# Opening loads: the first gate weights on ScalarE's DMA queue behind a memset, both first x tiles on SyncE's

## The chip, the cores and the metric

One core of a Trainium2 chip; the three sets of experiments ran on three different chips, each set with the kernel before beside it. The metric is the device time of one execution in microseconds (us). The span in a profile, first to last instruction, is about 1.8 us shorter than the time of the same execution. Medians and numbers of runs are given; where a ratio is given, it is the mean time of one kernel's fast runs over that of the other's of the same rounds, so not quite the ratio of the medians. A tile is 128 rows of x. A transfer is issued when the engine named starts it on its queue, and has landed at the last of its completion events in the trace.

## The reference

```python
xn = layernorm(x)                                  # x: 2048 x 640
g  = silu((sigmoid(xn @ w_gate) * (xn @ w_up)) @ w_down)   # F = 1536
s  = attention(xn @ wq, last 512 of k_cache, v_cache) @ wo # 32 heads of 192
return x + s * g
```

The kernel computes the gate part first. Only its first 16 us matter here: the first four tiles of 128 rows of x are loaded, normalized, transposed on TensorE and multiplied with the first 512 columns of the gate and up weights.

## The kernel before

```python
        nc.vector.memset(warm[:], 0.0)
        load_x(0, 1)                                   # SyncE's queue
        load_x(1, 1, nc.scalar)                        # ScalarE's queue, after a memset in the tile
        load_f(nc.sync, wg_sb, wg_r, 0, 4, 0, 3)       # gate part a, 384 KB
        load_f(nc.sync, wg_sb, wg_r, 0, 4, 3, NCD)     # gate part b, 256 KB
        load_f(nc.sync, wu_sb, wu_r, 0, 4, 0, 3)       # up part a, 384 KB
        load_x(2, 1)
        load_f(nc.sync, wu_sb, wu_r, 0, 4, 3, NCD)     # up part b, 256 KB
        load_x(3, 1)
        # ... rest of the weights and of x, on SyncE's queue
        nc.vector.memset(eps_t[:], eps)
        nc.scalar.activation(junk[:], eps_t[:], AF.Sqrt)
        # ...
    def stats_end(t):                                  # inside it, for tile 0:
            nc.scalar.activation(rstd[:], mv[:, 1:2], AF.Sqrt, bias=eps_t[:], scale=1.0)
            stats_half(1, 0)                           # x1's first statistics, ahead of...
            nc.vector.reciprocal(rstd[:], rstd[:])     # ...tile 0's reciprocal, in DVE's order
        # ...
        dummy(18)                                      # products on zeros while x0 is loaded
        dummy(6, 64)
        # ... statistics, normal(0), turn_pe(0): transposes of tile 0 on TensorE
        m0 = tile_gates(0, 3)      # 20 gate products, 12 up products, transposes of tile 1, 8 up products
        m1 = tile_gates(1, 1)
```

The transposes go to PSUM and from there to SBUF, by VectorE (DVE) and ScalarE for tile 0 and by ScalarE alone for the others; I call this the eviction.

The softmax here doesn't subtract the row's maximum and nothing guards it: scores larger than these inputs give would overflow.

## Time and profile before

| | before |
|---|---|
| median of 3 runs | 921.94 us (921.9 to 922.63) |
| span of the profiled execution | 920.8 us |
| TensorE busy | 914.8 us |
| first gate product | 6.20 us |
| first product of row tile 1 | 9.33 us |
| first product with 512 columns | 16.58 us |

The last three rows are start times of matmul groups in the timeline. I call the third one the **start of the stream**: from there on TensorE has all it needs, so an opening that is shorter by some amount makes that number smaller by the same amount. The prediction shows the lines of the profile.

### The profile page before, as it was taken

The numbers are of one execution on the slowest core, as the hardware profiler recorded it, in microseconds if no ns is written. First come the engines' busy times: TensorE is split into PE (matmuls) and PEld (weight loads), VectorE is DVE, ScalarE is ACT, GpSimd is POOL, SyncE is SP. The second block draws the span as 40 slices with busy tenths as digits, with TensorE's granted clock in tenths as the row PEclk, the third lists the DMA queues.
The fourth block names the chain that finished last, engine by engine and source line by source line (L and its number), as shares of the span: only waits on it lengthen the run. The fifth ranks groups of instructions, "written<-read, shape, count | busy, mean of one in ns | idle before, by whom it ended". The sixth has DMA issues, their size and how long they took to land.

```text
span 920.8 us, 25187 instructions
## 1 busy us (share of the span) xinstructions
PE 914.8 (99%) x11444; PEld 629.1 (68%) x11462; DVE 491.2 (53%) x982; ACT 302.3 (33%) x333; POOL 133.5 (15%) x158
## 2 busy tenths in 40 slices
PE   9999999999999999999999999999999999999998
PEld 7445455466868686767676777777776767686875
DVE  5452522445646464645555555545564646464677
ACT  4222222254142424233333333242414151515150
POOL 1000100001002000200120011001100111075633
PEclk9999999999999999999999999999999999999999
DMA  9320340115344434342426162616251615263535
GB/s 322 79 30 1 89 86 1 43 62 87 75 67 105 87 56 84 93 99 42 98 79 113 36 104 79 113 28 113 65 105 46 117 61 90 67 120 104 90 79 137
DMA packets 163147, 77.14 MB, mean 84 GB/s; under 512 B 140992, under 2 KB 158608, under 8 KB 163040
## 3 DMA queue, kind: packets, MB, share of 16 engines
q1 hardware_dynamic: 155936, 53.85, 29.9%
q0 software_dynamic: 5808, 20.52, 7.9%
q8 instruction: 89, 1.46, 0.7%
q10 hardware_dynamic: 1296, 1.16, 0.4%
q14 instruction: 18, 0.15, 0.1%
HBM read 39.45 MB, written 2.62 MB: 46 GB/s over the span
## 4 chain that ended last, share of the span: by engine, by line
PE 98%; DMA 1%; DVE 0%; SPq 0%; issue 0%; DVEq 0%
PE bank L494 22%; PE bank L423 21%; PE bank L445 19%; PE bank L405 18%; PE bank L251 10%; PE bank L263 6%; PE bank L371 1%; PE bank L301 1%; DMA wu_sb<-in_B_w_up_dram 1%; PE bank L529 0%; DVE o_sb L475 0%; DVE gate L480 0%; SPq L166 0%; SPq L161 0%; PE bank L231 0%
## 5 line engine op out<-in xcount | busy, mean ns | idle before, releaser
L409 ACT ACTIVATE E<-bank 128x1024 bf16<-128x1024 f32 x256 | 255.3, 1022 | 456.7 <-PE bank L405 456.6
L423 PE MATMUL bank<-xnT,wq_sb 64*128 64x512 bf16 x1800 | 226.4, 376 | 0.0
L494 PE MATMUL bank<-wo_sb,oT 64*128 64x320 bf16 x2688 | 205.2, 296 | 0.0
L405 PE MATMUL bank<-qT,kT 64*128 64x512 bf16 x1536 | 200.7, 376 | 0.0
L445 PE MATMUL bank<-vbuf,E 64*128 64x193 bf16 x4096 | 195.5, 243 | 0.0
L445 PEld LDWEIGHTS <-E 64*128 64x128 bf16 x4096 | 178.8, 94 | 10.4 <-issue 0.5
L494 PEld LDWEIGHTS <-oT 64*128 64x128 bf16 (+1 forms) x2892 | 163.3, 94 | 30.8 <-issue 0.5
L430 DVE CAST qT<-bank 128x1024 bf16<-128x1024 f32 x90 | 110.2, 1224 | 128.5 <-PE bank L423 128.5
L423 PEld LDWEIGHTS <-wq_sb 64*128 64x128 bf16 x1800 | 106.0, 100 | 87.1 <-issue 0.4
L405 PEld LDWEIGHTS <-kT 64*128 64x128 bf16 x1536 | 88.1, 94 | 73.5
L458 DVE TENSOR_TENSOR o_st<-bank,rden 128x768 bf16<-128x768 f32 x128 | 122.5, 957 | 4.8 <-DMA out_dram<-gate 0.4
L509 DVE TENSOR_TENSOR acc<-bank,acc 128x640 f32<-128x640 f32 x96 | 79.0, 823 | 20.3 <-PE bank L494 20.3
L118 POOL DMA_DIRECT2D vbuf<-in_A_v_cache_dram x28 | 21.1, 753 | 312.7 <-PE bank L445 309.8
L428 DVE COPY seen<-bank 128x2 f32<-128x2 f32 x90 | 14.3, 159 | 79.1 <-PE bank L423 79.1
L457 DVE RECIPROCAL rden<-bank 128x4 f32<-128x4 f32 x128 | 23.3, 182 | 60.6 <-PE bank L445 59.8
L251 PE MATMUL bank<-xnT,wg_sb 128*128 128x512 bf16 x216 | 54.5, 379 | 0.2
L251 PE MATMUL bank<-xnT,wu_sb 128*128 128x512 bf16 x215 | 54.4, 379 | 0.3
L257 DVE TENSOR_TENSOR hT<-bank,sig 128x512 bf16<-128x512 f32 x44 | 30.3, 689 | 42.7 <-ACT sig L254 42.7
L263 PE MATMUL bank<-wd_sb,hT 128*128 128x128 bf16 (+1 forms) x376 | 52.4, 297 | 0.4
L254 ACT ACTIVATE sig<-bank 128x512 bf16<-128x512 f32 x44 | 26.3, 597 | 68.4 <-PE bank L251 65.3
L263 PEld LDWEIGHTS <-hT 128*128 128x128 bf16 x384 | 29.7, 98 | 23.1
L251 PEld LDWEIGHTS <-wu_sb 128*128 128x128 bf16 x220 | 21.5, 98 | 26.0
(56 smaller groups left out, 366.6 us busy)
## 6 DMA issues: line engine op xcount, KB each, us to landing
wo_sb<-in_A_wo_dram SPq DMA_DIRECT2D x7, 960.0 KB, 5.5
wq_sb<-in_A_wq_dram POOLq DMA_DIRECT2D x7, 960.0 KB, 6.0
k_st<-in_A_k_cache_dram POOLq DMA_DIRECT2D x14, 384.0 KB, 5.4
vbuf<-in_A_v_cache_dram POOLq DMA_DIRECT2D x28, 192.0 KB, 3.6
row<-in_A_x_dram POOLq DMA_DIRECT2D x16, 160.0 KB, 2.8
oT<-o_st SPq DMA_TRANSPOSE x128, 3.4
x_sb<-in_A_x_dram SPq DMA_DIRECT2D x3, 640.0 KB, 9.9
wd_sb<-in_B_w_down_dram SPq DMA_DIRECT2D x1, 1920.0 KB, 13.5
```

The costliest lines, as they stand in the source:

```text
L251: nc.tensor.matmul(bank[k][:, half, 0:r1 - r0], lhsT=w[:, c, f * P:(f + 1) * P], rhs=xnT[:, b, c, r0:r1], start=(c == 0), stop=(c == NCD - 1))
L254: nc.scalar.activation(sig[:, 0:r1 - r0], bank[k][:, 0, 0:r1 - r0], AF.Sigmoid)
L257: nc.vector.tensor_tensor(hT[b][:, f, r0:r1], bank[k][:, 1, 0:r1 - r0], sig[:, 0:r1 - r0], ALU.mult)
L263: nc.tensor.matmul(wide(k)[:, d0:d1], lhsT=hT[b][:, f, q * P:(q + 1) * P], rhs=wd_sb[:, f, d0:d1], start=(f == 0), stop=(f == NF - 1))
L405: nc.tensor.matmul(bank[k][:, i, :], lhsT=kT[r, pr, j, c * P:(c + 1) * P], rhs=q[r, pr * DJ + j, :], start=(j == 0), stop=(j == DJ - 1))
L409: nc.scalar.activation(E[u, pr][:, c, :, :], bank[k][:], AF.Exp, scale=scale_qk)
L423: nc.tensor.matmul(bank[k][:, half, :], lhsT=wq[r, c, col:col + DJ * (P - 1) + 1:DJ], rhs=xnT[r, b, c, :], start=(c == 0 and not second), ...
L430: nc.vector.tensor_copy(qT[u][:, 2 * m:2 * m + 2, :], bank[k][:])
L445: nc.tensor.matmul(o4[:, q, 0:DH + 1], lhsT=e[r, c, h % 2, q * P:(q + 1) * P], rhs=vbuf[r, h, c, 0:DH + 1], start=(turn == 0 and qq == 0 a ...
L458: nc.vector.tensor_tensor(o_st[u][:, :, h * DH:(h + 1) * DH], o4[:, :, 0:DH], rden[:].to_broadcast([P, TQ, DH]), ALU.mult)
L494: nc.tensor.matmul(res[:, half, :], lhsT=oT[u][r, cc, q * P:(q + 1) * P], rhs=wo[r, cc, half * HD:(half + 1) * HD], start=(turn == 0 and c ...
L509: nc.vector.tensor_tensor(cols(acc[:, t, :]), res, cols(acc[:, t, :]), ALU.add)
```

## The change

Its intent is to let the first gate weights leave early from a queue of their own, without overtaking the first x tile, and to keep x in order on the other. The memset in the weight tile is only a gate: ScalarE's DMA has to wait for it.

```diff
-            if eng is nc.scalar:
-                nc.vector.memset(x[:, 0, 0:2], 0.0)
-            eng.dma_start(x[:], ...)
+            nc.sync.dma_start(x[:], ...)
         nc.vector.memset(warm[:], 0.0)
+        nc.vector.memset(eps_t[:], eps)
+        nc.vector.memset(wg_sb[:, 0, 0:2 * P], 0.0)
         load_x(0, 1)
-        load_x(1, 1, nc.scalar)
-        load_f(nc.sync, wg_sb, wg_r, 0, 4, 0, 3)
+        load_x(1, 1)
+        load_f(nc.scalar, wg_sb, wg_r, 0, 4, 0, 3)
...
-        nc.vector.memset(eps_t[:], eps)
         nc.scalar.activation(junk[:], eps_t[:], AF.Sqrt)
```

More of the change, by code (lines that the diff above doesn't have):

```diff
@@ L153, with load_x @@
         xt = {}
-        def load_x(t, n, eng=nc.sync):
+        def load_x(t, n):
             x = xpool.tile([P, n, D], BF16, name=f"x_sb{n}", bufs=4 if n == 1 else 2)
-            if eng is nc.scalar:
-                nc.vector.memset(x[:, 0, 0:2], 0.0)
-            eng.dma_start(x[:], xf[t * P:(t + n) * P, :].rearrange("(q p) d -> p q d", p=P))
+            nc.sync.dma_start(x[:], xf[t * P:(t + n) * P, :].rearrange("(q p) d -> p q d", p=P))
             for i in range(n):
```

## The prediction

> **What bounds the kernel now.** I read the page first, then the chain of waits, then the opening alone (the timeline, the weight loads, the waits, the DMA). The page settles the scale of everything that follows:
>
> ```profile
> span 920.8 us, 25187 instructions
> PE 914.8 (99%) x11444; PEld 629.1 (68%) x11462; DVE 491.2 (53%) x982; ACT 302.3 (33%) x333; POOL 133.5 (15%) x158
> PE 98%; DMA 1%; DVE 0%; SPq 0%; issue 0%; DVEq 0%
> ```
>
> TensorE is recorded busy for 914.8 of 920.8 us, and 98% of the chain that ended last is matmuls. All other time together is 6.0 us, 0.65% of the span. The change touches no matmul; it can only move the moment at which TensorE starts its useful stream without a further stop. So the question is where that moment is decided. The chain of the first 60 us says so, in order of time (start, length, what):
>
> ```profile
> 0.74 0.40 SPq L161
> 1.14 0.05 issue
> 1.20 0.42 SPq L166
> ...
> 2.70 0.63 SPq L161
> 3.33 0.04 issue
> 3.37 5.41 DMA wu_sb<-in_B_w_up_dram
> 8.78 0.05 issue
> 8.83 2.00 PE bank L301 x32
> ```
>
> SyncE issues the opening loads one after another. The sixth on its queue is the second part of the first up weights (row groups 3 and 4 of wu, 256 KB). It is issued at 3.37 and lands 5.41 us later, at 8.78; from there on the chain is TensorE to the end of that view. The weight loads of TensorE in the same stretch show the only two stops after the first useful product:
>
> ```profile
> 5.97 1.33 PEld L301 LDWEIGHTS <-wg_sb 128*128 128x128 bf16 x20
> 7.62 0.67 PEld L301 LDWEIGHTS <-wu_sb 128*128 128x128 bf16 x12 [0.32 <-DMA wu_sb<-in_B_w_up_dram]
> 8.25 0.32 PEld L231 LDWEIGHTS <-xn 128*128 128x128 bf16 x5
> 8.82 0.23 PEld L301 LDWEIGHTS <-wu_sb 128*128 128x128 bf16 x4 [0.25 <-DMA wu_sb<-in_B_w_up_dram]
> ```
>
> The gate weights, which the change moves, stop nobody: TensorE begins on them at 5.97 with no wait in brackets. It is the up weights behind them that it waits for, 0.32 and 0.25 us, **0.57 us in all**. Before 5.97 it does dummy products and the transposes of the first rows, which hang on the chain x row 0, statistics, square root, normalization.
>
> **What sets the landing at 8.78** is bandwidth. The DMA view of two stretches, 1.5 to 3.5 us and 3.5 to 9 us, has these lines (first pair, second pair):
>
> ```profile
> DMA packets 409, 0.45 MB, mean 226 GB/s; under 512 B 32, under 2 KB 409, under 8 KB 409
> q10 hardware_dynamic: 144, 0.16, 24.7%
> ...
> DMA packets 1956, 1.97 MB, mean 358 GB/s; under 512 B 96, under 2 KB 1956, under 8 KB 1956
> q1 hardware_dynamic: 1956, 1.97, 107.2%
> ```
>
> q10 is the queue that carried one x row tile (0.16 MB), so ScalarE's; q1 is SyncE's. From 3.5 us one queue alone fills the 16 engines at 358 GB/s. Before that there is a ramp, which the table by stretches gives second by second (stretch, length, busy times, clock, DMA share, GB/s):
>
> ```profile
> 1.50:2.50 1.00, 1.00 (x6) 0.72 (x5) 0.00 (x0) 1.00 (x1) 0.00 (x0) 1.00 0.58 150
> 2.50:3.50 1.00, 1.00 (x7) 0.72 (x5) 0.37 (x1) 0.48 (x2) 0.00 (x0) 1.00 0.93 302
> 3.50:4.50 1.00, 1.00 (x7) 0.69 (x6) 0.97 (x4) 0.21 (x1) 0.00 (x0) 1.00 1.06 369
> ```
>
> Only the ramp leaves transfer capacity unused; and the granted clock is 1.00 throughout.
>
> **What the Trainium skill says.** "DMA: Bandwidth & Descriptors", section "Issuing engines are not separate DMA queues": DMAs from any issuing engine run on the same 16 DMA engines and interleave; using several only saves sequencer time. The trace agrees: 358 GB/s with q1 alone, so a second queue adds no rate there. The same page, "Queues, rings and completion order": each DMA engine takes turns between the queues that hold work, packet by packet. This trace has both queues only briefly, and fits it without proving it. "Perfetto Trace Analysis", section "DMA Instruction — HWDGE (DVE, Sync)": the recorded issue ends once descriptors are made and leaves the data movement out. The trace agrees: the issue of the first gate weights takes 0.42 us, their landing 3.6 us.
>
> **The change part by part.**
> Order on SyncE. Before: x0, gate part a (384 KB), gate part b (256 KB), up part a, x2, up part b, x3. After: x0, x1, gate b, up a, x2, up b, x3. Up part b is still the sixth issue; an x issue of about 0.40 us stands where a gate issue of 0.42 us stood. Gain in issue time: 0.02 us, nothing.
> Constants. The two-element memset of x1 (0.06 us) goes; eps is set earlier (0.06 us, moved); a memset of 128x256 bf16 in wg_sb comes, and the one of the same size on warm took 0.17 us. DVE is idle until x0 lands at 3.1 us, so its 0.1 us more costs nothing there. It serves as a gate: ScalarE may issue gate part a only after it. From the memsets at 0.84 to 1.02 I put its end at about 1.15 and ScalarE's issue at about 1.2, where before ScalarE issued x1 at 1.06 and SyncE issued gate a at 1.20. So gate a starts when it did.
> ScalarE. Its table load for Sqrt moves from 1.50 to about 1.7 and, at 1.28 us plus 0.20 us for the first activation, ends near 3.2. The real square root is at 4.29, after DVE's statistics. Hidden.
> Bytes. Everything up to and with up part b is the same: three x tiles, 2x384 and 2x256 KB, 1.80 MB. At 358 GB/s from 3.5 us that stays the same. What may improve is the ramp: x1 and gate a now leave from two queues together instead of gate a waiting behind x0 in one. If 2.5 to 3.5 us ran at 358 instead of 302 GB/s, 56 KB more would be through, worth 56/358 = 0.16 us (an estimate). Up part b would land at about 8.6 instead of 8.78, and TensorE would stop 0.16 us less. Sum: **921.94 - 0.16, about 921.8 us**.
>
> **The rivals.**
> Gate weights late. Gate a now shares with SyncE's queue. By equal turns it is through when itself and as many packets of x1 and gate b are: about 0.79 MB from 2.6 us on at 358 GB/s, 2.2 us, so 4.8. From last byte to landing the trace before has 0.55 us for gate a and about 1.5 us for up b (1.80 MB less the 0.45 MB moved by 3.5 us, at 358, ends at 7.3; landed 8.78). So gate a lands between 5.4 and 6.3 instead of 4.8, needed at 5.97. At worst a new wait of 0.3 us appears; but TensorE would then reach the up weights 0.3 us later, where it stood waiting 0.32 us anyway. The total stays at 921.9. Quite likely in part.
> x1 late. It moves behind x0 on one queue and shares with gate a. DVE reaches x1's first statistics at 4.17, ahead of the reciprocal for row 0, so a late x1 would delay the first transposes. It landed at 1.06+2.4 = 3.5; I expect 3.8 to 4.1. If 0.5 us late, the first product moves to 6.5, and after the absorbed 0.3 us some 0.2 to 0.4 us remain: 922.2 to 922.4.
> Faster start of all. x0 no longer shares with x1, so its statistics may begin 0.1 us sooner. That helps nothing, since up part b is what ends last. Even if all weights were there in time, the ceiling is the two waits, 0.57 us: 921.4.
> TensorE's clock. A longer stop could lower the granted clock; with stops under 0.5 us and 1.00 in every stretch I see no sign.
>
> **Range and chances.** The mechanisms span 921.4 to 922.4. The three runs before spread from 921.9 to 922.63, so 0.7 us of scatter is as large as the whole effect, and upward. I take 921.2 to 922.6 for 8 in 10. Two per cent would be 18 us, 32 times the two waits together, and nothing after the first 10 us changes: practically certain to be the same.
>
> **What will show it.** In the profile of after: q10 with about 0.39 MB in place of 0.16; ScalarE issuing at about 1.2; the ramp from 2.5 to 3.5 us above 302 GB/s; the waits for the up weights still there but together below 0.57 us; the chain still through the DMA of up part b, landing near 8.6; after it the same matmul stream and the same PE busy time within 1 us. A wait for wg_sb before the first product, or for x1 on DVE near 4.2 us, would show a rival. The prediction is wrong if the first products begin over 0.5 us later, or if timing scatter between placements of the same stream exceeds what three runs showed.

## The result, and the profile after

| | before | after |
|---|---|---|
| median of 4 runs each | 922.08 us (921.9 to 922.63) | 922.40 us (922.24 to 924.55) |
| span of the profiled execution | 920.8 us | 920.5 us |
| first gate product | 6.20 us | 6.21 us |
| first product of row tile 1 | 9.33 us | 9.01 us |
| start of the stream | 16.58 us | 16.26 us |

The ratio is 1.0008 with a 95% interval of 0.9991 to 1.0025: the same. Times and traces point in opposite directions. The changed kernel's median is 0.3 us longer, yet its profiled execution is 0.3 us shorter, all of it gained by 9 us. One of its four runs took 924.55 us. It was not profiled, so its cause stays open.

The chain of waits of the changed kernel, first 60 us (start, length, what), no longer goes through the weights:

```profile
0.74 2.40 DMA x_sb<-in_A_x_dram
3.14 0.02 issue
3.17 0.90 DVE st L198 x2
...
6.21 1.95 PE bank L300 x32
8.15 0.29 PE bank L230 x5
8.45 0.02 issue
8.47 0.50 ACT xnT L236
8.97 0.04 issue
9.01 1.50 PE bank L300 x24
```

It now leads from the landing of x tile 0 over DVE's statistics to the first gate product, and then over the transposes of tile 1 (8.15) and their eviction on ScalarE (8.47 to 8.97) to the products of tile 1. TensorE's weight loads in the timeline show the same:

```profile
6.21 1.10 PEld L300 LDWEIGHTS <-wg_sb 128*128 128x128 bf16 x19 [0.33 <-issue]
7.26 0.71 PEld L300 LDWEIGHTS <-wu_sb 128*128 128x128 bf16 x12
7.93 0.32 PEld L230 LDWEIGHTS <-xn 128*128 128x128 bf16 x5
8.25 0.45 PEld L300 LDWEIGHTS <-wu_sb 128*128 128x128 bf16 x8
...
9.01 1.04 PEld L300 LDWEIGHTS <-wg_sb 128*128 128x128 bf16 x18 [0.25 <-issue]
```

Both waits for the up weights are gone (the brackets on the wu_sb lines are empty). The products of tile 1 start at 9.01 instead of 9.33, so only 0.32 of the 0.57 us came off. These lines of the kernel before show why:

```profile
8.78 0.77 ACT L237 ACTIVATE xnT<-bank 128x384 bf16<-128x384 bf16 x2 [2.40 <-PE bank L231]
...
9.33 1.28 PE L301 MATMUL bank<-xnT,wg_sb 128*128 128x128 bf16 x20
```

The first of the two evictions of tile 1 ran from 8.78 to 9.27 there, and tile 1's products followed at 9.33. It was level with the second wait (TensorE's eight weight loads behind that wait ran from 8.82 to 9.27), so taking that wait away on its own could gain nothing. b_amid2 and b_nowu below test this.

Two more views of the changed kernel contradict the prediction's working. The table by stretches gives the ramp:

```profile
2.50:3.50 1.00, 1.00 (x7) 0.72 (x5) 0.33 (x1) 0.66 (x2) 0.00 (x0) 1.00 0.90 228
```

The ramp got thinner, 228 GB/s where 302 had been and 358 was hoped for. Still the up weights came sooner. Here are the DMA lines of up part a, with the time from issue to landing at the end, first of the kernel before, then of the changed one:

```profile
wu_sb<-in_B_w_up_dram SPq DMA_DIRECT2D x1, 384.0 KB, 5.4
```

```profile
wu_sb<-in_B_w_up_dram SPq DMA_DIRECT2D x1, 384.0 KB, 4.9
```

Issued at 2.19 and 2.13 us, they landed at 7.58 and 7.04.

**The trace has one completion event for each of the 16 DMA engines of a transfer**, and these explain the difference. In the kernel before, 15 engines had finished up part a by 6.69 us and the last one at 7.58. The same lag stands in the transfers around it: gate part b 5.55 and 6.48, tile x2 7.14 and 8.03, up part b 7.89 and 8.78 (fifteenth and sixteenth engine). In the changed kernel the fifteenth and sixteenth finish up part a at 7.02 and 7.04. So the 8.78 us that I had put down to bandwidth was one engine 0.9 us behind the others. (The events do not name the engine. That it is the same one each time is inferred from the lag, which stays at 0.89 to 0.93 us.) The Trainium skill says in "DMA: Bandwidth & Descriptors", section "Why a DMA increments its semaphore by 16 and not by 1", that the engines of a transfer finish independently and that only the full count of 16 means landed. The trace agrees, and that last sixteenth is what TensorE waited for.

This left three questions. Is the lag an accident of one execution, or does it belong to the order of loads? Is the change slower by 0.3 us, as the times say, or faster by 0.3, as the traces say? What would the waits be worth if they were gone?

### The profile page after: what moved, and what is told of

The parts are those of the page before. It is cut to its first block, busy times and chain, and to the rows that moved or that the text cites. A ratio compares the mean times of both kernels' runs of the same rounds, so it can differ in the third digit from the quotient of the medians.

```text
span 920.5 us, 25205 instructions
## 1 busy us (share of the span) xinstructions
PE 914.9 (99%) x11462; PEld 631.0 (69%) x11462; DVE 491.3 (53%) x982; ACT 302.4 (33%) x333; POOL 133.7 (15%) x158
## 4 chain that ended last, share of the span: by engine, by line
PE 99%; DVE 1%; DMA 0%; ACT 0%; DVEq 0%; issue 0%
PE bank L493 22%; PE bank L422 21%; PE bank L444 19%; PE bank L404 18%; PE bank L250 10%; PE bank L262 6%; PE bank L370 1%; PE bank L300 1%; PE bank L528 0%; DMA x_sb<-in_A_x_dram 0%; DVE o_sb L474 0%; DVE st L198 0%; DVE gate L479 0%; PE bank L230 0%; DVE xn L218 0%; ACT xnT L236 0%
## 5 line engine op out<-in xcount | busy, mean ns | idle before, releaser
L262 PE MATMUL bank<-wd_sb,hT 128*128 128x512 bf16 (+1 forms) x384 | 52.8, 299 | 0.0
```

Of the source, the lines that this page charges most:

```text
L262: nc.tensor.matmul(wide(k)[:, d0:d1], lhsT=hT[b][:, f, q * P:(q + 1) * P], rhs=wd_sb[:, f, d0:d1], start=(f == 0), stop=(f == NF - 1))
```

## The experiments

Each kernel ran five times, once of these with a profile. The kernel before ran nine times beside each of the three sets, with medians 922.67, 922.43 and 922.56 us.

### Both kernels again

**b_again**, the kernel before, unchanged.

> The kernel before, unchanged, for more executions and a second trace. Theory A (the lag is an accident of one execution): the trace of before showed one of the 16 DMA engines about 0.9 us behind the other 15 on the up weights; if that comes and goes, this trace has the two waits for the up weights (0.32 and 0.25 us in the first trace) gone or much smaller, and the first 512-column product starts near 16.3 instead of 16.58 us. Theory B (the lag belongs to the order of before): the waits are there again within 0.1 us. Time against before: 1.000 under both.

**a_again**, the changed kernel, unchanged.

> The changed kernel, unchanged. Theory A: no lasting difference, ratio to before 0.9997 to 1.0003, and some trace may show the lagging engine here too. Theory B: stream 0.3 us earlier than before in every trace, ratio about 0.9997. Rival C (the change is slower by 0.3 us through its thinner ramp, 228 instead of 302 GB/s from 2.5 to 3.5 us): ratio 1.0003 or more, median 922.3 or more beside 921.9 for before.

Medians: b_again 922.58 us (ratio 0.9998), a_again 922.26 us (0.9994, interval 0.9982 to 1.0007). In b_again the waits for the up weights were there again (0.30 and 0.20 us), and an engine lagged again: up part a was done on 15 engines at 7.16 and on the last at 7.78. Theory B held for the kernel before. But the changed kernel's start of the stream was 16.80 us in a_again, later than in either trace of the kernel before so far. Theory B, 0.3 us sooner in every trace, fell with that. The DVE lines of its timeline say why:

```profile
4.11 0.21 DVE L203 BATCH_NORM_AGGREGATE mv<-st 128x2 f32<-128x12 f32 x1
...
4.79 0.49 DVE L198 BATCH_NORM_STATS2 st<-x_sb 128x6 f32<-128x320 bf16 x1 [0.47 <-DMA x_sb<-in_A_x_dram]
...
5.20 0.15 DVE L208 RECIPROCAL rstd<-rstd 128x1 f32<-128x1 f32 x1
```

An engine lagged here too, but it held up tile x1, which landed at 4.77 instead of 4.07. x1's first statistics stand ahead of tile 0's reciprocal in DVE's order, so a late x1 delays tile 0. The reciprocal came at 5.20 instead of 4.66 and the first gate product at 6.74 instead of 6.21.

### What the second queue does, and what the memset does

**one_queue**: the new order with nothing on ScalarE's queue.

```diff
-        nc.vector.memset(wg_sb[:, 0, 0:2 * P], 0.0)
-        load_f(nc.scalar, wg_sb, wg_r, 0, 4, 0, 3)
+        load_f(nc.sync, wg_sb, wg_r, 0, 4, 0, 3)
```

> The changed order, but the first gate weights also on SyncE's queue (third there) and no memset to hold ScalarE back: nothing at all leaves from ScalarE's queue in the opening. If the second queue matters, the gate weights (landing 5.2 in the changed kernel) and all behind them land about 0.4 us later, up weights near 7.5, stream start near 16.6, +0.3 us. If it only saves issue time and the engines are the limit, landings stay within 0.2 us and the time within 0.1 us.

Median 923.00 us, against 922.26 for the changed kernel in the same rounds. The gate weights were issued at 1.66 instead of 1.18, as third on the queue, and landed at 6.27. TensorE then waited for them, and again for the up weights:

```profile
6.31 1.19 PEld L299 LDWEIGHTS <-wg_sb 128*128 128x128 bf16 x20 [0.67 <-DMA wg_sb<-in_B_w_gate_dram]
8.18 0.67 PEld L299 LDWEIGHTS <-wu_sb 128*128 128x128 bf16 x12 [0.67 <-DMA wu_sb<-in_B_w_up_dram]
```

The stream started at 17.14. Up part a landed at 8.13, 1.09 us later than in the changed kernel's first trace. Of this, 0.24 us is the median engine (7.03 instead of 6.79), which goes with the issue slot of 0.45 us ahead of the weights; the rest is the lag of the last engine (1.10 us instead of 0.25). The times show no loss against the kernel before: the ratio is 1.0003 (interval 0.9991 to 1.0016). Both kernels save one slot by putting one transfer on ScalarE's queue. The change only swaps which.

**no_gate**: the changed kernel without the memset.

```diff
-        nc.vector.memset(wg_sb[:, 0, 0:2 * P], 0.0)
```

> The changed kernel without the memset that holds ScalarE's issue back until the constants are set: ScalarE then issues the gate weights at about 0.75 us, together with SyncE's first x row. If the memset is needed, the first x row shares the ramp with the gate weights, lands 0.3 to 0.8 us later than 3.14, and the first transposes (5.29) and the stream (16.26) follow by as much: +0.3 to +0.8 us. If it is not needed, x row 0 lands within 0.1 us of 3.14 and the time stays within 0.1 us or gains up to 0.3.

Median 924.13 us, 1.9 us more than the changed kernel in the same rounds. That is far beyond the 0.3 to 0.8 expected. ScalarE issued the gate weights at 0.74, together with SyncE's first. x0 landed at 3.50 instead of 3.14 and x1 at 5.05 instead of 4.07. The DVE lines show both waits, and TensorE's loads show an effect that I had not counted on:

```profile
3.52 0.89 DVE L197 BATCH_NORM_STATS2 st<-x_sb 128x6 f32<-128x320 bf16 x2 [2.51 <-DMA x_sb<-in_A_x_dram]
...
5.08 0.49 DVE L197 BATCH_NORM_STATS2 st<-x_sb 128x6 f32<-128x320 bf16 x1 [0.43 <-DMA x_sb<-in_A_x_dram]
...
6.82 2.28 PEld L299 LDWEIGHTS <-wg_sb 128*128 128x128 bf16 x20
```

Twenty gate loads took 2.28 us; nineteen took 1.10 in the changed kernel. TensorE was at half clock: the trace's record of clock changes has full speed from 9.74 us here and from 4.25 in the changed kernel. The first gate product was 0.85 us late (7.05 instead of 6.21) and the start of the stream 2.13 us late (18.39 instead of 16.26). All five runs (923.03 to 925.28) are longer than all five of the changed kernel in the same rounds (921.94 to 922.81): the memset is needed. In this trace the late x tiles are what its absence did. Whether the late clock also comes from it, or from chance, one trace does not show.

### Moving the transposes of tile 1

**a_amid2** and **b_amid2**: the same edit in the changed kernel and in the one before. The transposes of tile 1 come after 8 up products instead of 12.

```diff
-        m0 = tile_gates(0, 3)
+        m0 = tile_gates(0, 2)
```

> The changed kernel with the transposes of row tile 1 one row group earlier (after 8 up products instead of 12). Theory: with the up weights there in time, what TensorE waits for before its second row tile (9.01 us in the changed kernel) is the eviction of those transposes on ScalarE (8.47 to 8.97). Moved 4 products (0.22 us) ahead, the second row tile starts at about 8.8 and the stream at about 16.0 instead of 16.26: -0.2 us in the trace, ratio to the changed kernel 0.9998. Rival (the second parts of the weights bind): no change, second row tile at 9.0.

> The same edit in the kernel before. The prediction said that the landing of the second up weights (8.78) set the end there. If so, the edit gains nothing (up to 0.06 us), second row tile at 9.3 us. If the transposes' eviction alone was the limit (8.78 to 9.28, started by the late first up weights), it gains 0.2 us. With a lagging engine both are level in the traces of before, so I expect less than 0.1 us in an execution with a lag of 0.9 us and 0.2 us in one without.

In the trace of a_amid2 tile 1's products started at 8.93 and the stream at 16.19, 0.07 us sooner than in the changed kernel and not the 0.2 expected. A wait of 0.24 us for up part b took the freed place. b_amid2 happened to have a short lag: up part a landed at 7.31, before TensorE asked for it at 7.36. This is its opening:

```profile
7.36 0.45 PEld L301 LDWEIGHTS <-wu_sb 128*128 128x128 bf16 x8
...
8.55 0.45 PEld L301 LDWEIGHTS <-wu_sb 128*128 128x128 bf16 x8 [0.24 <-DMA wu_sb<-in_B_w_up_dram]
8.95 1.10 PEld L301 LDWEIGHTS <-wg_sb 128*128 128x128 bf16 x19
```

The stream started at 16.26, as in the changed kernel, but with the order of before. So the eviction of tile 1 and the second up weights are two paths of nearly the same length; shortening one exposes the other within 0.1 to 0.2 us. The medians, 922.56 and 922.39 us beside 922.43 for the kernel before, show no gain.

### x1 off the critical path, in two ways

**a_x1act**: x1 back on ScalarE's queue, the gate weights behind it there.

```diff
-        nc.vector.memset(wg_sb[:, 0, 0:2 * P], 0.0)
-        load_x(1, 1)
+        load_x(1, 1, nc.scalar)      # with the two-element memset of the kernel before
         load_f(nc.scalar, wg_sb, wg_r, 0, 4, 0, 3)
```

> x row 1 back on ScalarE's queue, ahead of the first gate weights there; SyncE has x0, gate b, up a and so on, one issue less ahead of the up weights. If issue order is what matters, up a is issued at about 1.7 instead of 2.13 and lands up to 0.4 us sooner (6.6), x1 lands near 3.5 as in before (spare time 0.7 us ahead of its statistics at 4.2) and the gate weights near 5.2. Since the up weights are no longer waited for in the changed kernel, its best time stays (stream 16.2 to 16.3), but executions where x1 came late (4.77 in the second trace of the changed kernel, stream 16.8) go: smaller scatter, median 0 to 0.3 us below. Rival: gate part b passes gate part a, part a lands after 5.9, a new wait of 0.2 us or more.

Median 924.11 us, ratio 1.0023 (interval 1.0010 to 1.0036), the only ratio whose interval leaves out 1. The rival named in the expectation came true. Gate part b, on SyncE's queue, landed at 4.21, and part a, which is needed first, at 7.37:

```profile
7.41 1.12 PEld L301 LDWEIGHTS <-wg_sb 128*128 128x128 bf16 x20 [1.53 <-DMA wg_sb<-in_B_w_gate_dram]
```

From 4.25 to 7.0 us the packets of both queues ran mixed in this trace, so part a shared the engines with up part a, which was not needed yet. In the changed kernel part a was issued before gate part b, and from 3.75 to 4.25 only its packets ran. The stream started at 17.49 in this trace, 0.91 us later than in the first trace of the kernel before, in a run of 923.5 us. The two longest runs (925.49 and 926.79 us) have no trace; their mean granted clock was 0.998 and 0.996, where every other run shows 0.999 or 1.000. So part of the loss in the median may be clock, and not the late gate weights.

**a_x1off**: x1's first statistics behind tile 0's normalization.

```diff
             nc.scalar.activation(junk[:], eps_t[:], AF.Sigmoid)
-            stats_half(1, 0)
             nc.vector.reciprocal(rstd[:], rstd[:])
...
         normal(0, ((0, 3 * P), (3 * P, D)))
+        stats_half(1, 0)
         stats_half(1, 1)
```

> The changed kernel with the first statistics of x row 1 taken out from ahead of row 0's reciprocal and put behind row 0's normalization. If a late x1 costs the changed kernel time through DVE's order (second trace: x1 at 4.77, reciprocal at 5.20 instead of 4.66, first transposes at 5.82 instead of 5.29), then here the first transposes stand near 5.25 whatever x1 does. x row 1's own chain starts 0.45 us later, so its normalized rows come near 8.0 instead of 7.59, its transposes near 8.1 instead of 7.93: in an execution with x1 in time 0.1 to 0.2 us slower, in one with x1 late 0.3 us faster; median within 0.2 us.

Median 922.49 us, with five runs within 0.28 us, the narrowest of all. x1 was late in its trace (4.45), and the first transposes stood at 5.16 all the same, as expected. But both statistics (0.88 us) now lay ahead of DVE's eviction of tile 0, which came at 6.05 instead of 5.81, and the first gate product at 6.44 instead of 6.21. The gain was given back there, a step that I had not listed.

### More runs, and no up weights in the first tile

**a_third** and **b_third**: both kernels unchanged once more.

> The changed kernel once more, for its scatter: medians so far 922.4 (4 runs) and 922.26 (5 runs), before 922.08, 922.67, 922.43. If the change gains the 0.3 us by which its first trace starts the stream sooner, median near 922.2 with before near 922.5. If it gains nothing, medians agree within 0.1 us. A trace with the stream start between 16.1 (no late transfer) and 16.7 (a late one).

> The kernel before once more. Stream start between 16.1 (no lagging engine) and 16.7 us (lag, waits for the up weights of 0.3 and 0.2 us), median 922.4 to 922.7.

Medians: a_third 922.31 us (ratio 0.9997), b_third 922.81 us (1.0002), the kernel before in the same set 922.56. Both traces are as expected, with the stream from 16.39 and from 16.63 us.

**a_nowu** and **b_nowu** (wrong results): the first row tile takes the gate weights for its up products, so that it cannot wait for the up weights.

```diff
-            for half, w in ((0, wg_sb), (1, wu_sb)):
+            for half, w in ((0, wg_sb), (1, wu_sb if t else wg_sb)):
```

> Wrong result on purpose: in the changed kernel the first row tile's up products take the gate weights, which are there already, so nothing in the first row tile can wait for the up weights. They are first needed at about 10 us, after their landing. Theory: in the changed kernel these waits are gone already in an execution without a lag, so the stream starts at 16.1 to 16.3 as before, time within 0.1 us of the changed kernel.

> The same in the kernel before, wrong result on purpose. It measures what the two waits for the up weights (0.32 and 0.25 us, 0.57 together) are worth. The prediction's ceiling: 0.57 us less, stream start 15.85. My theory now: the second is level with the eviction of row tile 1's transposes, so only the first comes off: second row tile at about 9.0 instead of 9.33, stream start 16.1, 0.3 us less in the trace; in the median of runs 0.1 to 0.3 us less, as not every execution has the lag.

Medians 922.43 and 922.88 us: nothing gained. b_nowu measures the disputed cost. The waits were gone and tile 1's products started at 9.15 instead of 9.33: 0.18 us came off, not the 0.57 of the prediction's ceiling. But this execution had the largest lag of all: tile x2 was done on 15 engines at 7.40 and on the last at 8.56, and TensorE stopped for its transposes:

```profile
8.58 0.89 DVE L199 BATCH_NORM_STATS2 st<-x_sb 128x6 f32<-128x320 bf16 x2 [0.98 <-DMA x_sb<-in_A_x_dram]
...
11.10 0.28 PEld L231 LDWEIGHTS <-xn 128*128 128x128 bf16 x5 [0.62 <-DVE xn L219]
```

The stream started at 17.03. Taking the wait for the up weights away did not take the lag away; it met the next consumer. In a_nowu TensorE's clock became full only at 6.94 us and its 32 first loads took 2.30 us, so the stream started at 16.67 and not at 16.1 to 16.3.

### All traces of the two orders

Every row is one execution. Lag is the time from the median to the last of the 16 engines on up part a. The last column runs from the start of the stream to TensorE's last weight load.

| trace | x1 landed | up a landed | lag | full clock from | tile 1 products | stream | stream to last load |
|---|---|---|---|---|---|---|---|
| before | 3.49 | 7.58 | 1.02 | 5.99 | 9.33 | 16.58 | 900.03 |
| b_again | 3.44 | 7.78 | 1.25 | 6.70 | 9.52 | 16.78 | 900.58 |
| b_third | 3.48 | 7.63 | 0.88 | 5.77 | 9.38 | 16.63 | 900.29 |
| after | 4.07 | 7.04 | 0.25 | 4.25 | 9.01 | 16.26 | 900.00 |
| a_again | 4.77 | 7.45 | 0.68 | 4.72 | 9.54 | 16.80 | 900.02 |
| a_third | 4.37 | 7.07 | 0.26 | 5.42 | 9.14 | 16.39 | 900.10 |

b_amid2 and b_nowu share the order of loads of before; up part a landed at 7.31 and 8.10 there, with lags of 0.85 and 1.54. a_amid2, a_x1off and a_nowu share that of the changed kernel, with 7.24, 7.49 and 7.22 and lags of 0.42, 0.78 and 0.52. Over five traces of the old order and six of the new one, up part a landed at 7.68 and 7.25 us on average (means of the landings just listed and in the table), and x1 at 3.48 and 4.35 (3.48 and 3.51 in b_amid2 and b_nowu; 4.13, 4.45 and 4.30 in a_amid2, a_x1off and a_nowu).

That is what the change did to the loads. **It brought the up weights 0.4 us sooner and x tile 1 0.9 us later.** DVE asks for x1 at about 4.2 us. In the old order it had 0.7 us to spare; in the new one it landed after 4.2 in 4 of 6 traces (in one of these, a_x1off, DVE asks for it only at 5.25). The gain on one path is partly spent on the other. Over the three traces of each unchanged kernel the stream started at 16.66 and 16.48 us on average, with single values from 16.26 to 16.80. Full clock also came earlier in the three traces of the changed kernel, but that is not the gain: in the kernel before the first gate product came no later (6.20, 6.17 and 6.18 us), and TensorE then stood waiting for the up weights.

The lag did not vanish in the new order; it stood elsewhere. On x1 the last engine was 0.12 to 0.27 us behind the median one in the five traces of the old order, and 0.39 to 1.16 in the six of the new one. That is 0.6 of the 0.9 us by which x1 came later; the median engine accounts for the rest (3.31 and 3.58 us on average). Nor does a second queue by itself take the lag off the up weights: on up part a it was 1.27 us in no_gate and 0.92 in a_x1act, beside 1.10 in one_queue.

## Why the prediction was right or wrong

**The size class was right**, and the reason for it: the change touches the first 10 us of a kernel whose rest is matmuls. The stream takes 900.0 to 900.6 us from its start in all six traces of the two unchanged kernels.

**The number**: 921.8 us was predicted, with 921.2 to 922.6. The median in the rounds of the result is 922.40, inside the range but on the other side of the kernel before. The ratio of means, 1.0008 on a mean of 922.17 for the four runs before (the average of the four), gives 922.9, outside the range by 0.3 us. This comes from the one run of 924.55 us. Over all runs the medians are 922.58 for the kernel before (41 runs, 921.90 to 924.12) and 922.32 for the changed one (14 runs, 921.94 to 924.55), so 0.26 us faster; the means differ by 0.16 us (922.62 and 922.46). These pool several sets and chips, and no set shows it beyond its interval: a gain is possible, but not shown.

**The step that failed first was "What sets the landing at 8.78 is bandwidth."** Fifteen engines had up part b by 7.89; one lagging engine made it 8.78. The same bytes at the same rate therefore did not mean the same landing. The prediction's own sums held the sign of it: from last byte to landing it had 0.55 us for gate part a and about 1.5 for up part b, and passed over the difference of 0.95, which is close to the lag of 0.89. The lag on up part a was 0.85 to 1.54 us in five traces of the old order and 0.25 to 0.78 in six of the new one. Why the new order carries less of it there is open. The packet records do not name the engine, and no run here chooses it.

**"56/358 = 0.16 us" from a fuller ramp failed in sign.** The stretch from 2.5 to 3.5 us carried 228 GB/s instead of 302. In the trace after, the first packets of gate part a ran only from 2.94 us, 1.8 us after their issue at 1.18, and x1's packets were spread until 3.7. The 16 engines were not idle meanwhile (a share of 0.90, after 0.93): single x packets of that stretch took up to 0.65 us, where the median packet of the opening took 0.05. Two queues at once did not fill the ramp. The median engine had up part a 0.2 us later than before (means of the engines' medians: 6.57 in five traces of the old order, 6.77 in six of the new one). The gain came from the lag alone. That up part b landed sooner, as predicted, was luck: the reason given for it was wrong.

**"Up part b is what ends last" was half right.** Up part b landed 0.57 us sooner (8.78 and 8.21), but the stream started 0.32 us sooner. The eviction of tile 1's transposes was level with it, and the view of the chain names one path alone. The two amid2 runs and b_nowu show the second and the third path.

**The rival "x1 late" came true in a_again**, with x1 0.7 us later than in the first trace of the changed kernel. Its first step, 0.5 us on the first product, came out at 0.53. Its second, that 0.3 us of it would be absorbed by the wait for the up weights, did not: that wait was gone, and the stream started the full 0.53 us later. I named this rival but gave it no weight in the central number. The rival "gate weights late" did not stop TensorE in the three traces of the changed kernel as it is: part a landed at 5.17, 5.60 and 5.86, inside my 5.4 to 6.3 or just ahead of it. In a_amid2 and a_x1off it landed at 6.04 and 6.05, and the weight load then waited for it, level with the eviction of tile 0.

**"The granted clock is 1.00 throughout" was a misreading.** The trace of the kernel before has its first clock record, full speed, at 5.99 us, and the view prints 1.00 for the time before it too. The dummy products of 256 columns show what ran there: in both kernels one started every 0.21 us, and in the changed kernel every 0.11 us once its record says full speed (4.25). So the rival on the clock was put aside on a number that said nothing about the opening. It did not decide the result's two traces (first gate product at 6.20 and 6.21), but it moved the stream in no_gate and a_nowu.

**The scatter was set too small.** It was taken from three runs, 0.7 us in all. The kernel before later ranged over 2.2 us in 41 runs. Three sources are visible in the traces: the lagging engine, the instant at which TensorE's clock becomes full, and up to 0.6 us somewhere between the start of the stream and the end.

No variant beat both kernels beyond the scatter. None of the orders tried gained more than some tenths of a microsecond, and two of them (no_gate, a_x1act) lost 1.5 and 1.7 us in the median against the kernel before in the same rounds.

## What to carry to other kernels

Read a late landing by the completion of every DMA engine before you put it down to bandwidth: one engine 0.9 us behind looks the same in a chain of waits. Where several paths of an opening end within 0.3 us of each other, a chain names one of them, and taking its wait away mostly shows the next; estimate such a gain by the second-longest path. And before predicting tenths of a microsecond, take the scatter from more than three runs, or predict from a landmark in the trace, such as the start of the stream, which moved by 0.3 us between the first two traces where the times could not tell (it too scattered, by 0.2 and 0.5 us over three traces of each kernel).

## What the Trainium skill lacked or had wrong

- "DMA: Bandwidth & Descriptors", section "Issuing engines are not separate DMA queues", says that a second issuing engine only saves sequencer time, usually small beside the transfer. The first part holds (358 and 359 GB/s from 3.5 to 9 us in the two profiles). The second is not contradicted: the slot is about 0.45 us beside a landing of 4.9 us. What the section lacks is a size for an opening: in one_queue the median engine had up part a 0.24 us later, while most of the later stream (17.14 us instead of 16.26) is lag.
- The same page has no size for how far the last DMA engine of 16 can lag behind the median one: on a 384 KB transfer from SyncE's queue it was 0.85 to 1.25 us in the traces of the kernel before and of b_amid2, 1.54 in b_nowu, and 0.25 to 0.78 in six traces of the new order.
- "TensorE: Matmul & The Clock Gate", section "Part 1: The HAM clock gate (the "warmup" mystery)", gives the change to full clock at about 4 us into sustained work, ±500 ns between runs. Here, with the first product at 1.06 us every time, it came between 4.25 and 6.70 us in six traces of the two kernels, 3.2 to 5.6 us after the start; and at 9.74 us in no_gate, where TensorE had stopped for 0.70 us ahead of the first transposes.
- No page says that a chain of waits hides paths of nearly equal length: here 0.57 us of recorded waits were worth 0.32 in the first pair of traces.
